# Two of VectorE's weight sums and two of the v transfers in a fused HGRN2 and SwiGLU kernel stand elsewhere

## Chip, core and metric

The kernel runs on one core of a Trainium2 chip. The metric is the device time of one execution in microseconds (us), the median of three runs. The core has five engines that run side by side, each with a queue of its own: TensorE (PE) for matrix products, VectorE (DVE) and ScalarE (ACT) for elementwise work, GpSimd (POOL), which here clears small pieces and issues DMAs, and SyncE (SP), which only issues DMAs. Engines wait for one another by semaphores. On-chip data lie in SBUF, and products arrive in PSUM, in eight banks.

## The reference

Two blocks follow each other. The first is a gated linear recurrence over 768 steps for 4 sequences and 8 heads of size 48; the second is a SwiGLU feed-forward block on the 3072 rows that result.

```python
f = 1.0 / (1.0 + np.exp(-f_logit))
for t in range(S):
    state = f[:, :, t, :, None] * state + np.einsum('bhd,bhe->bhde', k[:, :, t], v[:, :, t])
    y[:, :, t] = np.einsum('bhd,bhde->bhe', q[:, :, t], state)
x = y.transpose(0, 2, 1, 3).reshape(B * S, H * D)     # 3072 x 384
g = x @ w_gate                                        # 384 x 1536
out = (g * (1.0 / (1.0 + np.exp(-g))) * (x @ w_val)) @ w_out
```

Inputs q, k, v and f_logit are float32; the three weight matrices come as 64-bit floats and are turned into 32-bit ones on the chip.

## The kernel before

The 768 steps are cut into six chunks of 128, and a chunk of one sequence is a unit: unit u = 4c + b is chunk c of sequence b. In a unit the recurrence becomes matrix products: scan the gates along the chunk, scale k and q by them, form the scores (k times q, line 666), mask them causally (line 681, tile A), multiply by v (lines 706 and 727, into y), and carry the state on (lines 747 and 756). The feed-forward block runs chunk by chunk too, on the 4 x 128 rows of one chunk. So while the products of chunk c run, the attention of chunk c + 1 is woven in between.

There are three stages. The first does the attention of chunk 0 alone. The middle stage (until about 143 us in the profile) does the feed-forward of chunk 0 plainly (lines 802 and 825) with the attention of chunk 1, and turns the weights into 32 bits piece by piece: w_gate and w_val first, w_out last (join, line 501). The third stage does chunks 1 to 5, each as a block. In a block the hidden layer is computed as a 3 x 3 by 3 x 2 block product with 15 products in the place of 18: `mlp_fifteen` runs the 15 products of `PRODUCTS` four times (line 1004). Groups of products accumulate in one bank each (A, B, o, c). ScalarE copies a bank out between two products of the same letter (line 1009), VectorE adds and subtracts the copies (`plus`, line 905, and `minus`, line 908), ScalarE applies Silu (line 1020), and VectorE multiplies the halves into h (line 956). The copies that VectorE only adds go into three buffers called aside. Then `down_seven` multiplies h by w_out as a 2 x 2 block product with seven products (line 1103 and line 1166). It needs four sums of the halves of w_out, ws1, ws2, w_out's own upper right half, and ws4, which `down_weight_sums` makes once, in the first block of this kind, that is the second of all (chunk 1):

```python
return [lambda: minus(down_sums[1], b12, b11), lambda: minus(down_sums[2], b22, down_sums[1]),
        lambda: minus(b12, b22, b12), lambda: minus(down_sums[4], b21, down_sums[2])]
```

Each is one VectorE operation on 128 x 1152 float32 elements.

In the third stage the order on every engine is the program order, written out by hand: `in_order` at its end ties each engine's instructions together. The order comes from a plan with due times. Each product counts 0.86 of a nominal time unit and each of the seven down products 3.9; a list `waiting` holds the steps of the attention, the sums of tokens and the four weight sums with their due times, and before each product everything that is due is emitted. `DOWN_SUMS_AT` (line 901) holds the due times of the four sums, counted from the start of block 1. The steps of the attention have theirs from `SCORES`, `CHAINS` and `times`. For the unit 9, the gate transpose (line 604) is due at 13.2 and its masks at 26.65; for the unit 10 the gate transpose is due at 28.7. What VectorE has to do with a product's result is emitted one product later (`lag`).

The attention reads its inputs in two ways. Units 0 to 5 load q, k and f in rows and TensorE turns them. From unit 6 on (`by_squares`) the inputs are laid out in 32 x 32 squares, four transfers for each input, which VectorE transposes itself (lines 604, 614, 652). v is always loaded in rows, 128 rows of eight pieces of 48 elements. `load` (line 431) issues the transfers: for chunks 2 and later all from SP; for units 6 and 7, the two units by squares in chunk 1, the squares of f, k and q from GpSimd (line 447) and v from SP (line 454). On SP, v of these units stands among the weight transfers (line 471) and the transfers of y (line 717) of the middle stage. `keep_order(by_pool[-5:])` ties the squares' transfers on GpSimd together.

Of the kernel before, what the change touches and what calls it, by code (L numbers as in the profile page):

```python
# [290 lines left out]
def short_path(ctx, tc, ident, least, judge, q, k, v, f_logit, moe_w_gate, moe_w_val, moe_w_out, out):  # L291
# [9 lines left out]
    nc = tc.nc  # L301
    B, H, S, D = q.shape
# [13 lines left out]
    SQUARES = 2  # L316
# [84 lines left out]
    def by_squares(u):  # L401
        return u >= SQUARES * B - 2
# [6 lines left out]
    def v_of(u):  # L409
        return vs[u % (NV if units[u][1] < SQUARES else NV // 2)]  # L410
# [20 lines left out]
    def load(u, what="fkqv"):  # L431
        b, c = units[u]
        rows = slice(c * C, (c + 1) * C)
        inputs = dict(f=f_logit, k=k, q=q, v=v)
        for nm in "fqkv" if c >= SQUARES else "fvkq" if by_squares(u) else "fkqv":
            src = inputs[nm]
            if nm not in what:
                continue
            if nm == "v":
                dst = v_of(u)  # L440
            elif not by_squares(u):
                dst = raw[nm][u % NRAW]
            else:
                since = len(traced)
                for n in range(4):
                    at = Q * (1 - n % 2)
                    (nc.sync if c >= SQUARES else nc.gpsimd).dma_start(
                        out=rooms[nm][Q * n:Q * (n + 1), at:at + HP * RUN].rearrange("t (a e) -> t a e", a=HP),
                        in_=src[b, n // 2::2, rows, :].rearrange("a (t i) d -> t a (i d)", i=NI))
                if c < SQUARES:  # L450
                    by_pool.extend(ins for ins in traced[since:] if ins.engine == mybir.EngineType.Pool)
                    keep_order(by_pool[-5:])
                continue
            nc.sync.dma_start(out=dst[:, :, 0:D], in_=src[b, :, rows, :].rearrange("h t d -> t h d"))

    def weight_piece(dst, src, parts):

# [97 lines left out]
    def attention(u):  # L555
# [69 lines left out]
        if not in_squares:  # L625
            kp = transposed("kTp", kr)
            qp = transposed("qTp", qr)
            if by_squares(u + 1):
                load(u + 1)
# [120 lines left out]
        if c >= SQUARES and u + 2 < len(units):  # L750
            load(u + 2, "v")
# [7 lines left out]
    def load_after(u, what):  # L759

        if u + 1 < len(units) and u + 1 != SQUARES * B:
            load(u + 1, what)
# [16 lines left out]
    def keep_order(mine):  # L779
        for a, b in zip(mine, mine[1:]):  # L780
            tc.add_manual_dep(b, a.name, mybir.DependencyInfo(mybir.DependencyClass.NoSync,
                                                              mybir.DependencyReason.DATA), reason="order")
# [115 lines left out]
        return {"o": banks_o, "A": banks_a}[kind].tile([128, 512], FP32, tag=kind, name="sc")  # L898

    FINISH = (3, 5, 6, 7, 9, 10)  # L900
    DOWN_SUMS_AT = (28, 34, 38, 48)
    sums = {}

    def plus(dst, a, b):
# [31 lines left out]
    def down_weight_sums():  # L936

        DH = DM // 2
        b11, b12 = w_out[:, 0:NP, 0:DH], w_out[:, 0:NP, DH:DM]
        b21, b22 = w_out[:, NP:NF, 0:DH], w_out[:, NP:NF, DH:DM]  # L940
        for i in (1, 2, 4):
            down_sums[i] = comb.tile([128, NP, DH], FP32, tag=f"ws{i}", name=f"ws{i}")
        return [lambda: minus(down_sums[1], b12, b11), lambda: minus(down_sums[2], b22, down_sums[1]),
                lambda: minus(b12, b22, b12), lambda: minus(down_sums[4], b21, down_sums[2])]
# [364 lines left out]

    waiting += [(at, f) for at, f in zip(DOWN_SUMS_AT, down_weight_sums())]  # L1310
    blocks = {}
# [26 lines left out]
def kernel(  # L1338
# [22 lines left out]
    def judge(bank):  # L1361
# [13 lines left out]
        yield  # L1375

    short_path(tc, ident, least, judge, *args)
    with tc.If(redo[0] > 0, label="redo"):
        general_path(tc, *args)
# [32 lines left out]
```

## Time and profile before

| | |
|---|---|
| median of 3 runs | 604.13 us (604.05 to 604.21) |
| profiled execution | 605.36 us |
| its span, first to last instruction | 603.5 us |
| mean granted TensorE clock | 0.995 |
| second block, 144 to 240 us | VectorE busy 84.0 us, ScalarE 49.0 us |
| VectorE, L908 ws<-w_out and ws<-w_out,ws | 3 operations, 1.33 to 1.35 us each |
| VectorE, L908 w_out<-w_out | 1 operation, 1.35 us |
| v transfers from SP | 24 of 192 KB, 2.7 us from issue to landing (median) |
| squares of f, k, q of units 6 and 7 from GpSimd | 24 of 96 KB |

The span is what the profiler saw between the first and the last instruction; the execution's own time has 1.86 us around it. A row of the order of time gives the start, the duration, the engine, the source line, the operation, the tiles written and read, and in brackets how long the engine sat idle before it and what released it. On VectorE the drawn durations overlap a little: the next operation starts 0.05 to 0.1 us before the drawn end of the one before. The end of a matmul is modelled.

Where the pieces stand in the profile: the four sums start at 176.15, 185.92, 193.30 and 199.84 us; v of unit 6 is issued from SP at 78.20 and v of unit 7 at 99.97. TensorE reads them from 116.65 (unit 6) and 131.00 (unit 7) on.

### The profile page before, as it was taken

Reading aid. Unit: us, or ns where it says so; the run is one execution under the profiler, and the core shown is the slowest. Engines: PE = TensorE matmul, PEld = TensorE weight load, DVE = VectorE, ACT = ScalarE, POOL = GpSimd, SP = SyncE. Lnnn points to the kernel's source line nnn. Section 1 sums busy time; section 2 is a strip of 40 time slices with the busy share of each in tenths; the row PEclk is TensorE's granted clock in tenths of the full one; section 3 lists DMA queues with packets and bytes.
Section 4 is the critical chain, followed back from the end, with each engine's and each line's share of the span. In section 5 each row is a group of like instructions: output and inputs, shape, how many; then the busy total and the mean of one; then the engine's idle time right before and its main releaser. Section 6 shows DMA issues by size and latency. Waiting matters only on the chain.

```text
span 603.5 us, 10851 instructions
## 1 busy us (share of the span) xinstructions
PE 591.9 (98%) x4004; PEld 487.6 (81%) x4004; DVE 480.3 (80%) x831; ACT 294.8 (49%) x559; POOL 86.2 (14%) x199
## 2 busy tenths in 40 slices
PE   7899999999999999999999999999999999999996
PEld 5754545667888899888899888899988899988896
DVE  7999997868999977998895978995878982666631
ACT  2577853215776521567631476742376730356600
POOL 1001251000030150030330030330030320000000
PEclk9999999999999999999999999999999999999999
DMA  9998682015322044342434333343240100100001
GB/s 197 243 294 286 199 211 63 5 35 157 80 63 69 17 129 124 102 114 65 115 103 109 116 91 71 87 110 101 85 105 26 28 9 6 53 1 1 1 1 55
DMA packets 105210, 56.28 MB, mean 93 GB/s; under 512 B 67136, under 2 KB 97216, under 8 KB 105152
## 3 DMA queue, kind: packets, MB, share of 16 engines
q1 hardware_dynamic: 97632, 46.49, 29.4%
q0 software_dynamic: 5504, 6.30, 3.5%
q10 hardware_dynamic: 2016, 2.75, 1.3%
q8 instruction: 32, 0.52, 0.4%
q14 instruction: 26, 0.21, 0.1%
HBM read 45.74 MB, written 6.82 MB: 87 GB/s over the span
## 4 chain that ended last, share of the span: by engine, by line
PE 93%; DVE 5%; issue 1%; ACT 0%; DVEq 0%; ACTq 0%
PE o L1103 19%; PE A L1004 16%; PE B L1004 13%; PE c L1004 5%; PE o L1004 5%; PE gate L802 5%; PE o L825 5%; PE val L802 5%; PE sc L666 4%; PE o L1166 3%; PE y L706 3%; PE y L727 2%; PE dS L747 2%; PE y L702 2%; PE kt L670 1%; DVE c L908 1%
## 5 line engine op out<-in xcount | busy, mean ns | idle before, releaser
L717 POOL DMA_DIRECT2D xT<-yT x120 | 59.9, 507 | 50.3 <-ACT yT L710 45.3
L1103 PE MATMUL o<-w_out,h 128*128 128x192 f32 x360 | 62.0, 327 | 0.5 <-DVE h L956 0.5
L1004 PE MATMUL A<-xs,w_both 128*128 128x256 f32 x240 | 62.2, 382 | 0.0
L1103 PEld LDWEIGHTS o<-w_out,h 128*128 128x128 f32 x360 | 58.7, 190 | 1.7 <-DVE h L956 0.8
L1009 ACT COPY c<-A 128x512 f32<-128x512 f32 x40 | 23.3, 583 | 59.5 <-PE A L1004 59.5
L1009 ACT COPY aside<-A 128x512 f32<-128x512 f32 x60 | 35.1, 586 | 33.7 <-PE A L1004 33.6
L905 DVE TENSOR_TENSOR c<-c,aside 128x512 f32<-128x512 f32 x60 | 41.1, 685 | 12.4 <-ACT aside L1009 11.0
L1004 PEld LDWEIGHTS A<-xs,w_both 128*128 128x128 f32 x240 | 44.9, 190 | 6.6
L956 DVE TENSOR_TENSOR h<-h,c 128x256 f32<-128x256 f32 x100 | 40.4, 412 | 7.3 <-ACT h L1020 7.1
L681 DVE TENSOR_TENSOR A<-sc,causal 128x512 f32<-128x512 f32 x48 | 30.9, 686 | 16.9 <-PE sc L666 16.9
L908 DVE TENSOR_TENSOR c<-c,aside 128x512 f32<-128x512 f32 x60 | 40.9, 682 | 2.8 <-ACT aside L1009 2.8
L1020 ACT ACTIVATE h<-c 128x256 f32<-128x256 f32 x100 | 39.2, 416 | 7.6 <-DVE c L905 5.7
L656 POOL MEMSET gates<- 128x4 f32 x24 | 3.3, 139 | 272.6 <-DVE qT L570 267.5
L1103 PE MATMUL o<-ws,h 128*128 128x192 f32 x240 | 41.5, 328 | 0.2 <-DVE A L681 0.2
L1004 PE MATMUL B<-xs,w_both 128*128 128x256 f32 x160 | 41.3, 380 | 0.1
L1004 PE MATMUL c<-xT,w_both 128*128 128x256 f32 x160 | 41.2, 380 | 0.1
L1004 PE MATMUL A<-xs,extra 128*128 128x256 f32 x160 | 41.2, 380 | 0.0
L1004 PE MATMUL B<-xT,extra 128*128 128x256 f32 x160 | 41.1, 379 | 0.0
L1009 ACT COPY aside<-B 128x512 f32<-128x512 f32 x60 | 35.1, 585 | 9.5 <-PE B L1004 6.6
L1103 PEld LDWEIGHTS o<-ws,h 128*128 128x128 f32 x240 | 39.1, 190 | 0.8 <-DVE A L681 0.4
L905 DVE TENSOR_TENSOR c<-c,o 128x384 f32<-128x384 f32 x15 | 8.3, 552 | 36.3 <-PE o L1103 36.3
L908 DVE TENSOR_TENSOR c<-o,c 128x512 f32<-128x512 f32 x40 | 27.4, 684 | 11.0 <-ACT h L1020 6.2
(149 smaller groups left out, 1221.0 us busy)
## 6 DMA issues: line engine op xcount, KB each, us to landing
fsquares<-in_f_logit_dram SPq DMA_DIRECT2D x64, 96.0 KB, 2.5
qsquares<-in_q_dram SPq DMA_DIRECT2D x64, 96.0 KB, 2.1
ksquares<-in_k_dram SPq DMA_DIRECT2D x64, 96.0 KB, 2.4
v<-in_v_dram SPq DMA_DIRECT2D x24, 192.0 KB, 2.7
w<-in_moe_w_gate_dram SPq DMA_DIRECT2D x6, 768.0 KB, 6.1
w<-in_moe_w_val_dram SPq DMA_DIRECT2D x6, 768.0 KB, 6.2
w<-in_moe_w_out_dram SPq DMA_DIRECT2D x6, 768.0 KB, 5.6
out_dram<-ob ACTq DMA_DIRECT2D x14, 192.0 KB, 2.0
```

The lines of the kernel that those rows point to most:

```text
L666: nc.tensor.matmul(sc[par][:, a * C:(a + 1) * C], lhsT=kT[r, a, :], rhs=qT[r, a, :], start=True, stop=True)
L681: nc.vector.tensor_tensor(A[:, par], sc[par].rearrange("p (a t) -> p a t", t=C), causal.unsqueeze(1).broadcast_to((128, HP, C)), ALU.mult)
L717: (nc.gpsimd if c >= SQUARES else nc.sync).dma_start(out=xT[c][f % 128:f % 128 + n, f // 128, b * C:(b + 1) * C], in_=yT[r:r + n, par, a / ...
L802: nc.tensor.matmul(p, lhsT=w[:, j, i, :], rhs=xT[c][:, i, :], start=(i == 0), stop=(i == KT - 1))
L825: nc.tensor.matmul(p, lhsT=hidden_tile(h, n // 2)[:, n % 2 * 2 + b // 2, b % 2 * C:(b % 2 + 1) * C], rhs=w_out[:, j, :], start=(n == 0), s ...
L905: nc.vector.tensor_tensor(dst, a, b, ALU.add)
L908: nc.vector.tensor_tensor(dst, a, b, ALU.subtract)
L956: lagging.append(lambda: f(*args))
L1004: nc.tensor.matmul(p[name][:, n, :], lhsT=weights_of[a][:, n, j, :], rhs=tokens[b], start=fresh and n == 0, stop=True, skip_group_check=True)
L1009: nc.scalar.copy(t, p[name])
L1020: nc.scalar.activation(dst, src[:, 0, :], AF.Silu)
L1103: nc.tensor.matmul(p[:, n, :], lhsT=lhsTs[j][:, n * C:(n + 1) * C], rhs=rhs[:, j, :], start=first and j == order[0] and n == 0, stop=j == ...
```

## The change

The first two due times of the weight sums become smaller, so that the first sum is emitted directly before the gate transpose of unit 9 and the second directly before the masks of unit 9; the third and fourth stay. And `load` takes GpSimd's queue for v where the unit goes by squares and its chunk is below `SQUARES` (2), that is for units 6 and 7; the order of the transfers in the program is as before (f, v, k, q).

```diff
@@ -451,7 +451,8 @@
                     by_pool.extend(ins for ins in traced[since:] if ins.engine == mybir.EngineType.Pool)
                     keep_order(by_pool[-5:])
                 continue
-            nc.sync.dma_start(out=dst[:, :, 0:D], in_=src[b, :, rows, :].rearrange("h t d -> t h d"))
+            queue = nc.gpsimd if c < SQUARES and by_squares(u) else nc.sync
+            queue.dma_start(out=dst[:, :, 0:D], in_=src[b, :, rows, :].rearrange("h t d -> t h d"))
 
@@ -898,7 +899,7 @@
     FINISH = (3, 5, 6, 7, 9, 10)
-    DOWN_SUMS_AT = (28, 34, 38, 48)
+    DOWN_SUMS_AT = (13.1, 26.5, 38, 48)
     sums = {}
```

## The prediction

> **What bounds the kernel now.** I read the busy times, then the waits of each engine, then the chain of waits, and last the order of time of VectorE (DVE) and TensorE (PE) around the places that the change touches.
>
> ```profile
> PE 591.9 (98%) x4004; PEld 487.6 (81%) x4004; DVE 480.3 (80%) x831; ACT 294.8 (49%) x559; POOL 86.2 (14%) x199
> ...
> 132.00:144.00 12.00, 12.00 (x57) 7.60 (x54) 10.10 (x21) 4.84 (x7) 0.24 (x3) 1.00 0.46 126
> 144.00:240.00 96.00, 95.06 (x701) 84.04 (x700) 84.01 (x140) 49.03 (x99) 15.49 (x35) 1.00 0.34 88
> 240.00:335.00 95.00, 95.00 (x708) 85.05 (x708) 81.76 (x144) 49.11 (x97) 16.53 (x36) 1.00 0.40 104
> ```
>
> TensorE is the bound, so only its holes are worth anything. By stage (start:end, length, busy time of PE, weight loads, DVE, ACT, POOL) it has none from 30 to 144 us and none from 240 to 518 us; outside the first 30 us and the last 85 us, the second block (144 to 240 us) alone has holes, 0.94 us of them. That is also the block of the four sums. The chain of waits shows what makes them:
>
> ```profile
> 186.00 1.25 DVE ws L908
> ...
> 188.28 0.59 ACT aside L1009
> ...
> 188.91 1.13 PE B L1004 x4
> ...
> 194.65 0.61 DVE c L908
> 195.26 0.04 issue
> 195.30 1.15 PE c L1004 x4
> ...
> 203.33 0.61 DVE c L905
> 203.94 0.02 issue
> 203.97 0.43 ACT h L1020
> 204.39 0.02 issue
> 204.41 0.44 DVE h L956
> ...
> 204.90 1.24 PE o L1103 x6
> ```
>
> From about 177.5 to 204.9 us the chain runs almost wholly on VectorE: its queue is behind, and TensorE meets the backlog three times (a bank not yet copied out at 188.91, a bank not yet read at 195.30, a part of h not yet multiplied at 204.90). Products start 0.865 us apart, so B was due at 187.77 + 0.865 = 188.635 and is 0.275 late; c was due at 194.20 + 0.865 = 195.065 and is 0.235 late; the down product was due at 201.59 + 16 x 0.1625 = 204.19 (7.80 us for 48 in the chain gives 0.1625) and is 0.71 late. After each hold the next product starts about 0.10 later than its pace (0.97 for 0.865, as after 188.91). Together 1.22 + 0.30 = 1.5 us: the most that a shorter queue on VectorE can bring here. It is more than the 0.94 of the busy times because part of a hold is drawn as a longer matmul.
>
> ```profile
> 157.94 1.12 DVE L604 STREAM_TRANSPOSE gates<-fsquares 128x512 f32<-128x512 f32 x1 [0.84 <-issue]
> ...
> 174.29 1.29 DVE L681 TENSOR_TENSOR A<-sc,causal 128x512 f32<-128x512 f32 x2 [1.41 <-PE sc L666]
> ...
> 176.15 1.35 DVE L908 TENSOR_TENSOR ws<-w_out 128x1152 f32<-128x1152 f32 x1
> 177.54 0.69 DVE L908 TENSOR_TENSOR c<-o,c 128x512 f32<-128x512 f32 x1
> ```
>
> VectorE is idle 0.84 us before the transpose at 157.94 (it waits for ScalarE's sigmoid, 157.22 to 157.85) and 1.41 us before the masks at 174.29. These are the two places that the sums move to.
>
> **What the Trainium skill says.** "VectorE: DVE Perf Modes", Mode 2×_2P: an operation on two tensors cannot use the second read port to go twice as fast; at the 0.96 GHz of its Specifications 1152 elements are 1.20 us, an estimate. The trace agrees: 1.33 to 1.35 drawn, 1.25 to 1.27 from start to the next start. "TensorE: Matmul & The Clock Gate", Architectural detail: VectorE's queue is strictly first in, first out. So an idle place is filled only by what stands ahead of the waiting instruction, which the gaps above show as well. "SBUF — State Buffer", SBUF: two separate sides: a DMA issued from GpSimd needs descriptors that GpSimd writes, and some VectorE operations keep it from that. The trace fits in size: the same four f transfers took 4.58 us of GpSimd at 58.05 and 2.20 at 78.44. "DMA: Bandwidth & Descriptors", Issuing engines are not separate DMA queues: another issuer saves only issue time; on SP that is 0.42 and 0.53 us for the two v transfers.
>
> **The change part by part.**
>
> *First sum, from 176.15 to ahead of the transpose.* VectorE's operation before it starts at 156.41 and gives way 0.60 later, at 157.01. The sum ends its turn at 158.28 (1.27), so the transpose starts 0.34 late. The next slack is at 163.39, where the addition waits for ScalarE's copy until 163.36; it takes up 0.18 and leaves 0.16. What TensorE needs from this queue next is ScalarE's copy of c at 166.23, held by the h product at 165.74: it would end at 166.98 instead of 166.82, and the product that needs it starts at 167.34. Nothing is lost on TensorE; without the slack at 163.39 the copy ends at 167.16, still in time. Where the sum stood, it is worth almost nothing: it ended at 177.50, and c<-o,c behind it also waits for the product o, which starts at 176.41 and ends 1.03 later, at 177.44. Gain there: at most 0.06, and the h product at 179.09 takes it back, since it starts when ScalarE's Silu ends (178.62 + 0.42 = 179.04).
>
> *Second sum, from 185.92 to ahead of the masks.* VectorE becomes free at 172.80 + 0.16 = 172.96; the sum ends its turn at 172.96 + 1.27 = 174.23, and the scores that the masks wait for come at 174.25. Cost nothing; if the whole 0.34 remained the masks would be 0.12 late, taken up by the idle time that now lies ahead of 177.48. Where it stood it is on the chain, 185.92 to 187.17 = 1.25 us. From there to 203.25 VectorE's starts follow each other at the pace of their kinds (0.60 for 512 elements, 0.33 for 256, 1.27 for the two other sums), so all of it comes 1.25 earlier unless something else is late first.
>
> *What is late next.* I moved the queue of 186 to 205 us forward by hand. ScalarE's copy that held B waits for the addition at 187.50 and for its product (185.91 + 1.03 = 186.94): it starts at 187.03 and ends at 187.62, before 188.635. Product c is due at 194.69; its bank is read out by 194.0. The next copies of A, B and c follow their products with 0.3 us and more to spare. So the first two holds go (0.375 + 0.335 with their restarts) and TensorE reaches the third at 204.19 - 0.71 = 203.48. The part of h comes at 204.90 - 1.25 = 203.65. TensorE still waits 0.17 there, and the gain at that point is VectorE's 1.25, not TensorE's 1.5. Behind it, TensorE, VectorE and ScalarE are all earlier by the same amount; the hold of 0.19 at 221.96 stays, because its mask follows its own scores. From 223 us on nothing holds TensorE, so the 1.25 reaches the end.
>
> *v of the two units.* SP loses two issues of 0.4 to 0.5 us; what follows there (the yT transfers at 93.66 and 117.80) waits for ScalarE. GpSimd gets them:
>
> ```profile
> 58.05 4.58 POOL L447 DMA_DIRECT2D fraw<-in_f_logit_dram  x4 [11.71 <-PE fTp L590]
> 73.62 2.18 POOL L447 DMA_DIRECT2D kraw<-in_k_dram  x4 [11.00 <-PE kTp L590]
> ...
> 87.75 2.34 POOL L447 DMA_DIRECT2D kraw<-in_k_dram  x4 [7.11 <-DVE qT L614]
> ```
>
> The trace has no v on this queue. From below: one issue like the others, 0.55. From above: v has 1024 runs of 192 bytes where one of these transfers has 128 of 768, so eight times 0.55 to 1.15, 4.4 to 9.2 us. A gain is excluded, since TensorE waits for nothing here. I take 2 us; it matters little. The first v falls into GpSimd's 11.00 idle after f; behind it k waits for 73.62 anyway. The second stands between k and q of unit 7, with the clearing of a gate column and nothing else behind; q is read at 110.29, some 14 us after it lands, and v itself at 131. Cost nothing at either end. If the cover were gone, q late by x would cost x less 14, less the 9.3 us between qT (114.2) and its scores (123.5).
>
> Sum: 605.36 (the profiled execution: span 603.5 and 1.86 around it) - 1.25 = 604.1. The median of the three runs lies 1.23 below that execution; the same step from 604.13 gives 602.9.
>
> **The rivals.**
>
> *Something else holds the third and fourth triples.* ScalarE or a buffer takes over part of the 1.25: the two small holds go, the last does not, or the reverse. For it: three holds of different kinds stand within 17 us, and ScalarE's margins are 0.3 to 0.6. Against: every margin I worked out is positive. Gain 0.4 to 0.9: about 603.5.
>
> *All holds go, also the last.* VectorE catches up 0.17 more than its pace shows. Gain 1.5: 602.6.
>
> *Both sums were hidden already.* True of the first, shown above. For the second it would need the h product at 187.17 to wait for ScalarE, whose Silu ended at 184.44: against. 604.1.
>
> *Slower: v's move lays out the middle stage anew.* Between 50 and 144 us the code pins the order of few instructions; the rest is placed by a planner that counts each queue's time. The trace shows that it does not keep program order (two matmuls of y at 112.92, the other fourteen at 116.06). If v's issue on GpSimd pushes the masks of the last unit (done at 127.07) behind later sums, y at 131.00 waits. Cover is 3.9 us; from a slip of 5.2 on the gain is gone. A slip of 7 us, as for ten sums of 0.60 and a join moved ahead, costs TensorE 7 - 3.9 = 3.1 us, less the 1.25 gained: 606.0. Against: v is needed late and no instruction of VectorE depends on it.
>
> **How the numbers follow.** Forecast 0.60, partial gain 0.19, all holds 0.06, nothing 0.05, slower 0.10. About 0.2% (1.2 us) is what a measurement of this kernel can tell from no change, and the forecast's own size, 1.25 with some 0.15 either way from the spacing of VectorE's turns, lies on that edge: I give 0.38 of its 0.60 to faster. Faster 0.38 + 0.06 + 0.02 of the partial = 0.46; slower 0.10; the rest, 0.44, is within. The range 602.3 to 604.4 leaves out the slower case and the tails.
>
> **What would show it.** Right: ws between 157.0 and 158.4 and again between 172.9 and 174.3, no idle time of VectorE at either place, a new one of about 1.3 us ahead of c<-o,c near 177.5; the products near 188.6 and 194.7 at their pace; h and TensorE's down product near 203.65; v on POOL behind f and between k and q. Wrong: a hold of TensorE between 157 and 174 us, a new wait of PE for ACT near 190 to 202, or any hole between 50 and 144 us.

## The result, and the profile after

| | before | after |
|---|---|---|
| median (16 runs of each) | 604.13 us (603.92 to 604.30) | 602.78 us (602.42 to 604.18) |
| ratio of the times | | 0.9982, 95% interval 0.9976 to 0.9989 |
| profiled execution | 605.36 us | 602.79 us |
| span | 603.5 us | 601.1 us |
| granted clock, mean | 0.995 | 0.999 |

The kernel became 1.35 us faster; the forecast was 1.2 faster (602.9). The profiles are 2.57 us apart, which is more than the medians, and the reason lies in the execution that was profiled before, not in the change. In the lines below (start:end, length, busy time of TensorE, weight loads, VectorE, ScalarE, GpSimd, granted clock, DMA) look at the clock, the third figure from the right. First the kernel before, then the kernel after:

```profile
28.00:30.00 2.00, 2.00 (x40) 1.60 (x34) 1.93 (x6) 1.08 (x3) 0.00 (x0) 0.50 0.87 186
30.00:32.00 2.00, 2.00 (x17) 1.27 (x14) 1.74 (x5) 1.47 (x5) 0.00 (x0) 0.65 1.05 333
```

```profile
28.00:30.00 2.00, 1.95 (x49) 1.49 (x50) 1.93 (x5) 1.39 (x4) 0.00 (x0) 1.00 1.03 210
30.00:32.00 2.00, 2.00 (x5) 0.92 (x6) 1.93 (x5) 1.68 (x4) 0.89 (x1) 1.00 0.89 315
```

For about 4 us the matmuls of that one execution ran at half to two thirds of their pace. Two kernels of the experiments below (the two sums alone, the first sum alone) have the same first stage and were profiled without such a dip; in both, the second block starts at 141.85 us, and in the profile of before at 143.20. So the dip cost 1.35 us, about the 1.23 by which the profile of before lay above its median, and which the prediction carried along without a cause. Most variants have some executions that are over 1 us longer at a lower mean clock; they were not profiled, so where their clock dipped is not shown.

So the second block is compared by its length, not by its place. In the chain of waits its first product, A, starts at 143.20 before and at 142.10 after (1.10 earlier), and the attention's y behind the first down products starts at 206.46 before and at 204.09 after (2.37 earlier). The block is 2.37 - 1.10 = 1.27 us shorter. Behind it almost nothing changes up to VectorE's last sum, which starts 2.39 earlier (598.43 and 596.04). Ahead of it something does: with v on SP and no dip the block starts at 141.85, and in the kernel after at 142.10, 0.25 later. That is v's doing, as the experiments show.

The stages of the kernel after, in the same columns:

```profile
144.00:240.00 96.00, 95.80 (x717) 85.20 (x716) 85.19 (x145) 50.65 (x102) 15.47 (x35) 1.00 0.34 85
240.00:335.00 95.00, 95.00 (x697) 85.27 (x697) 81.72 (x144) 47.84 (x96) 16.50 (x36) 1.00 0.40 103
```

The 0.94 us without matmuls in the second block have shrunk to 0.20. The chain of waits of the kernel after shows which are gone (start, length, engine, tile, line; lines are one further down than before):

```profile
187.69 0.86 PE B L1005 x4
188.56 0.86 PE o L1005 x4
...
192.87 0.86 PE B L1005 x4
193.74 0.86 PE c L1005 x4
...
198.91 1.00 PE A L1005 x4
199.91 2.60 PE o L1104 x16
202.51 0.01 issue
202.52 1.57 PE o L1104 x8
...
218.85 0.68 DVE A L682
219.54 0.04 issue
219.58 10.02 PE o L1104 x60
```

The long stretch of VectorE that filled the chain of before between 177.5 and 204.9 us is not there any more: B and c, late by 0.275 and 0.235 before, follow their predecessors at the pace of 0.86, and TensorE alone is the chain up to 218.85, where the mask holds it as it did before. At the down product the view shows no hold, and still a little of one is left. A matmul is drawn about 0.165 us into the next one (four are drawn 1.03 long and follow each other at 0.865), so a hold as short as that leaves no idle time in a view. It is seen by what follows: in the order of time TensorE's 24 down products begin at 199.75 and y at 204.02, 4.27 us for what takes 3.99 without a hold (199.39 to 203.38 in the experiment with three sums below). The 0.28 are the wait of 0.17 and the restart of 0.10 that the prediction left there.

VectorE, in order of time, at the places the sums moved to and the place the first one left:

```profile
155.92 1.35 DVE L909 TENSOR_TENSOR ws<-w_out 128x1152 f32<-128x1152 f32 x1
157.19 1.16 DVE L605 STREAM_TRANSPOSE gates<-fsquares 128x512 f32<-128x512 f32 x1
...
171.89 1.35 DVE L909 TENSOR_TENSOR ws<-w_out,ws 128x1152 f32<-128x1152 f32 x1
173.19 1.29 DVE L682 TENSOR_TENSOR A<-sc,causal 128x512 f32<-128x512 f32 x2
...
176.44 0.69 DVE L909 TENSOR_TENSOR c<-o,c 128x512 f32<-128x512 f32 x1 [1.31 <-PE o L1005]
```

Both sums stand with no idle time of VectorE before or behind them, and the idle 1.31 ahead of c<-o,c is new.

### The profile page after: what moved, and what is told of

Read it like the earlier page. It is cut to its first block, busy times and chain, and to the rows that moved or that the text cites. A ratio compares the mean times of both kernels' runs of the same rounds, so it can differ in the third digit from the quotient of the medians.

```text
span 601.1 us, 10855 instructions
## 1 busy us (share of the span) xinstructions
PE 589.4 (98%) x4004; PEld 486.0 (81%) x4004; DVE 480.5 (80%) x831; ACT 294.7 (49%) x559; POOL 87.7 (15%) x201
## 4 chain that ended last, share of the span: by engine, by line
PE 97%; DVE 1%; ACT 0%; issue 0%; ACTq 0%; DVEq 0%
PE o L1104 20%; PE A L1005 18%; PE B L1005 14%; PE c L1005 6%; PE o L1005 6%; PE gate L803 5%; PE o L826 5%; PE val L803 5%; PE sc L667 4%; PE o L1167 3%; PE y L707 3%; PE y L728 2%; PE dS L748 2%; PE y L703 2%; PE kt L671 1%; PE fTp L591 0%
```

## The experiments

All were timed beside the kernel before on the same chip (604.15, 604.06 and 604.09 us in three sessions, each on another chip). The sums are named by their place in `DOWN_SUMS_AT`.

**The two sums alone, v left on SP.**

```diff
-    DOWN_SUMS_AT = (28, 34, 38, 48)
+    DOWN_SUMS_AT = (13.1, 26.5, 38, 48)
```

> The two sums stand at their new places, v stays on SP. My theory (VectorE's backlog of 186 to 205 us is the whole gain): 602.9, that is 1.25 below before, and TensorE's holds at B and at c of the fourth triple gone. Rival (v brings part of the gain, by the queues of the first 60 us): 603.3 to 604.1.

602.74 us (602.64 to 603.03), ratio 0.9977 (0.9969 to 0.9986). The sums bring the whole gain: 1.41 us here, 1.35 with v on GpSimd.

**v alone.**

```diff
-            nc.sync.dma_start(out=dst[:, :, 0:D], ...
+            (nc.gpsimd if c < SQUARES and by_squares(u) else nc.sync).dma_start(out=dst[:, :, 0:D], ...
```

> v of units 6 and 7 goes from GpSimd, the sums stay where they were. My theory: 604.1, no change within 0.1, since nothing on TensorE waits for these transfers or for GpSimd. Rival (v is part of the gain): 602.9 to 603.7. Rival (v's earlier issue costs something in the crowded first 60 us): 604.4 or more, or more executions with a longer first stage.

603.9 us (603.75 to 607.0), ratio 1.0003 (0.9995 to 1.0011): no effect on the time that can be told. But the order of time shows that v is not where the prediction put it, and that its issue is not free. The kernel before, then v alone:

```profile
25.66 0.36 DVE L498 TENSOR_SCALAR top<-top 128x384 int32<-128x384 int32 x1
...
27.02 1.28 DVE L681 TENSOR_TENSOR A<-sc,causal 128x512 f32<-128x512 f32 x2
...
27.59 0.43 SPq L454 DMA_DIRECT2D v<-in_v_dram  x1
...
27.80 1.84 PE L727 MATMUL y<-A,v 128*32 128x128 f32 x32 [0.64 <-issue]
```

```profile
24.95 1.16 POOL L454 DMA_DIRECT2D v<-in_v_dram  x1 [4.49 <-PE dS L747]
25.29 0.35 DVE L496 TENSOR_SCALAR top<-top 128x384 f32<-128x384 f32 x1
...
25.67 0.60 DVE L498 TENSOR_SCALAR top<-top 128x384 int32<-128x384 int32 x1
...
27.28 1.28 DVE L681 TENSOR_TENSOR A<-sc,causal 128x512 f32<-128x512 f32 x2
...
28.07 1.19 PE L727 MATMUL y<-A,v 128*32 128x128 f32 x31 [0.90 <-ACT kt L679]
```

While GpSimd issues v of unit 6 (1.16 us), one VectorE operation beside it, of a weight piece, takes 0.60 instead of 0.36. The queue behind it is 0.25 late, with the masks and so the product y. (The trace puts y's wait down to ScalarE's kt, done at 27.85; the masks are what comes last.) The page "SBUF — State Buffer" of the Trainium skill states in its section Who interferes with whom that VectorE's modes with two ports, which operations of this kind (TENSOR_SCALAR) can enter, and GpSimd contend for a shared pair of ports: whoever starts first has it for the whole instruction, and the other blocks. The trace agrees in part: the operation that was held ends 0.16 after GpSimd's, but the one before it (25.29), which also started during the issue, was not held. That GpSimd's issue causes the delay is shown by the runs with one v each, below; that the ports are the way is not. The prediction had taken from that page only the other direction, VectorE keeping GpSimd waiting.

**The first sum alone.** `DOWN_SUMS_AT = (13.1, 34, 38, 48)`, v on SP.

> Only the first sum moves, ahead of the gate transpose; the second stays due at 34. My theory: the first sum was hidden behind the wait for product o, so 604.0 to 604.1, and the idle time of about 1.3 us ahead of c<-o,c near 177.5 shows it. Rival (each sum is worth half): 603.5.

604.14 us, ratio 1.0003 (0.9995 to 1.0011). VectorE's order of time there:

```profile
176.20 0.69 DVE L908 TENSOR_TENSOR c<-o,c 128x512 f32<-128x512 f32 x1 [1.31 <-PE o L1004]
```

The sum has gone, and VectorE stands idle for its whole length in the same place, since c<-o,c cannot start before the product o. TensorE is busy 20.25 of the 21 us from 185 to 206, as before. The first sum was hidden where it stood.

**Both sums directly ahead of the masks.** `DOWN_SUMS_AT = (26.4, 26.5, 38, 48)`, v on SP.

> Both sums stand directly ahead of the masks (due 26.4 and 26.5), none at the transpose. The gap there is 1.41 us and the two need 2.5, so the masks come 1.05 late, near 175.3; the wait for product o until 177.48 takes that up. My theory: 602.9, as with both moves. Rival (the place ahead of the transpose is needed for the first sum): 603.5 to 604.1.

602.84 us (602.64 to 603.14), ratio 0.9976 (0.9967 to 0.9985): as good as the change. VectorE, in order of time:

```profile
171.49 1.35 DVE L908 TENSOR_TENSOR ws<-w_out 128x1152 f32<-128x1152 f32 x1
172.87 1.36 DVE L908 TENSOR_TENSOR ws<-w_out,ws 128x1152 f32<-128x1152 f32 x1
174.15 1.28 DVE L681 TENSOR_TENSOR A<-sc,causal 128x512 f32<-128x512 f32 x2
...
176.23 0.69 DVE L908 TENSOR_TENSOR c<-o,c 128x512 f32<-128x512 f32 x1
```

The masks are 1.2 later than with the two places of the change (172.95) and take up the idle 1.31 that the first sum left behind; c<-o,c is where it was. So the place ahead of the transpose isn't needed. The second sum was not moved by itself; but both together gain 1.41 or 1.31 and the first alone nothing, so what counts is that the second leaves the stretch from 186 us on.

**The second sum done twice.** The kernel before, with the second sum repeated where it stands (the same values are written a second time).

```diff
-    waiting += [(at, f) for at, f in zip(DOWN_SUMS_AT, down_weight_sums())]
+    at_sums = list(zip(DOWN_SUMS_AT, down_weight_sums()))
+    waiting += at_sums + [(34.1, at_sums[1][1])]
```

> The kernel before, with the second sum done twice, one behind the other, at its old place. My theory: between 186 and 205 us TensorE follows VectorE's queue, so a sum more costs what a sum less gains: 1.25, so 605.4. Rival (the queue has slack that one more sum only uses up): 604.1 to 604.6.

605.5 us (605.26 to 606.62), ratio 1.0026 (1.0015 to 1.0037): 1.44 longer than before. TensorE, in order of time:

```profile
188.94 1.13 PE L1004 MATMUL B<-xs,w_both 128*128 128x256 f32 x4 [1.51 <-ACT aside L1009]
```

Product B, 0.275 late before, now waits 1.51 us, by the way the prediction named: sum, h and addition on VectorE, the copy of the bank on ScalarE, the product. A sum at this place costs about its own length of 1.25, taken away or added.

**The third sum moved as well.** `DOWN_SUMS_AT = (13.1, 26.5, 28, 48)`, v on SP, so that w_out's sum stands in the idle time that the first sum opened.

> Sums at their new places, v on SP, and the third sum is due at 28, in the idle time ahead of c<-o,c that the first one left. My theory: it fits there (1.27 into 1.31), VectorE's queue of 186 to 205 us is shorter by another 1.25, TensorE's last hold (0.17 and 0.10 with its restart) goes and nothing else is gained: 602.45, 0.27 below the sums alone. Rival (VectorE still sets the end of the block): 601.5. Rival (the sum pushes the gate transpose behind it): 602.7 or more.

602.5 us (602.25 to 604.66), ratio 0.9980 (0.9972 to 0.9987). VectorE and then TensorE in order of time, and the busy times by stage:

```profile
174.68 1.35 DVE L908 TENSOR_TENSOR w_out<-w_out 128x1152 f32<-128x1152 f32 x1
176.08 0.69 DVE L908 TENSOR_TENSOR c<-o,c 128x512 f32<-128x512 f32 x1
```

```profile
199.39 4.06 PE L1103 MATMUL o<-w_out,h 128*128 128x192 f32 x24
203.38 0.67 PE L702 MATMUL y<-qT,decayed 48*64 48x128 f32 x16
```

```profile
185.00:206.00 21.00, 21.00 (x147) 18.38 (x147) 20.07 (x34) 12.82 (x27) 0.11 (x1) 1.00 0.07 20
```

The third sum fills 1.3 us in which VectorE waited, the last of the three holds goes, and with it the 0.28 that were left. By the medians three sums are the fastest: 1.56 us below the kernel before, where the two sums alone are 1.41 and the change 1.35 below. The intervals overlap, so the size of this last step rests on the trace. A second timing, in another session, gave 602.58 (1.51 below; ratio 0.9973, 0.9964 to 0.9983):

> The same three sums with v on SP, for the comparison on one chip: 602.5 in both theories, y at 27.8, the window 185 to 206 us full on TensorE.

**v of one unit alone,** with the two sums of the change: `nc.gpsimd if u == 7`, and `nc.gpsimd if u == 6`.

> Sums at their new places, and only v of unit 7 goes from GpSimd. Seen so far: v of unit 6 is issued by GpSimd at 24.95 us for 1.16 us, and a VectorE operation at 25.67 takes 0.60 in the place of 0.36, so TensorE's y near 27.8 starts 0.25 later. My theory now: GpSimd's descriptor work for v of unit 6 holds VectorE, v of unit 7 (issued near 30.2) holds nothing that matters. So here y starts at 27.8, the last sum of VectorE at 595.8 as with the sums alone, time 602.7. Rival (any v on GpSimd costs, or gains, alike): y or the first stage moves here too.

> Sums at their new places, and only v of unit 6 goes from GpSimd. My theory: the VectorE operation at 25.67 takes 0.60, y starts at 28.05, the last sum stands at 596.0, all as in the changed kernel; time 602.7 to 602.9, and more executions with a dip of TensorE's granted clock near 28 us (1.2 us longer), since TensorE is idle 0.25 longer just ahead of it. Rival (the dips fall by chance): as rare as with the sums alone.

Unit 7 alone: 603.2 us (602.93 to 605.15); VectorE's operation at 25.65 takes 0.36 and y starts at 27.81, as before the change. Unit 6 alone: the operation takes 0.60 and y starts at 28.05. So v of unit 6 is what holds y. (Beside unit 7's issue a VectorE operation is longer too, 0.78 instead of 0.36 us at 30.36, but y is under way by then.) The times don't fit as well. Unit 7 alone is about 0.5 longer than the two sums alone, which were timed on another chip. Of unit 6 alone seven of 13 executions were 1.1 us or more above the rest, which makes its median 604.33, and the rest (603.09 to 603.25) is also 0.4 longer, though VectorE's last sum starts at 596.03, as in the change (596.04). From that sum to the end of the span the profiles have 4.8 to 5.6 us, another length in each kernel; part of the 0.4 lies there. What sets that end is open.

**Three sums with both v on GpSimd,** beside the same without.

> The third sum moved as well, with v of units 6 and 7 on GpSimd; the kernel beside it has the same sums with v on SP. Theory one (GpSimd's work for v of unit 6 holds a VectorE operation of the first stage by 0.24 us and with it y at 27.8): y about 0.25 later than in the kernel beside it, and a median 0.2 to 0.3 longer, 602.7 to 602.8 against 602.5, with more executions in which the granted clock dips near 28 us. Theory two (v costs nothing, as predicted): the same median within 0.1 and the same share of dips.

602.49 us (602.25 to 603.51), ratio 0.9971 (0.9960 to 0.9982), against 602.58. y starts at 28.06 and not 27.82, as the first theory says, but the median doesn't show it: of three pairs with and without v on GpSimd (change and sums alone 602.78 and 602.74, in different sessions; v alone and before 603.9 and 604.15; this pair) none is longer by more than 0.04. The profiles do show it up to VectorE's last sum. Here are the first sum alone, whose time is that of the kernel before and whose profile has no dip, and v alone:

```profile
597.08 0.35 DVE L905 TENSOR_TENSOR ob<-c,o 128x192 f32<-128x192 f32 x1 [1.59 <-PE o L1166]
```

```profile
597.36 0.35 DVE L905 TENSOR_TENSOR ob<-c,o 128x192 f32<-128x192 f32 x1 [1.59 <-PE o L1166]
```

With v on GpSimd the last sum is 0.28 later; between the sums alone and the change it is 0.22 (595.82 and 596.04), and in this pair 0.63. What comes behind the last sum is shorter with v on GpSimd in the first pair (5.22 and 4.84 us) and in this one (5.47 and 4.94) and takes most of it back; in the second (5.08 and 5.06) it is not, and there the profiled executions are 0.15 apart (602.64 and 602.79). In this kernel's profiled execution, 602.86 us long, TensorE also has one wait in the middle stage, which makes up the rest of the 0.63:

```profile
PE sc L667 <- ACT top L491: 0.3, 1, 0.3
```

The scores of unit 5 at 78.24 come behind a weight piece of ScalarE. Unit 7 alone had the same wait with 0.15, the change and unit 6 alone have none. Whether v causes it, by what it moves among the weight transfers, was not separated.

## Why the prediction was right, and where it was not

*The bound and the three holds.* Right. The gain is all in the second block, and the two holds that the forecast said would go are gone. One reading was off: the three holds, 1.22 together, show as less idle time not because a held matmul is drawn longer, but because each matmul of these products is drawn 0.165 into the next, so each hold shows about 0.16 less (0.11, 0.07 and 0.55; with the later 0.19 these are the 0.94 within 0.02).

*First sum, nothing; second sum, 1.25.* Right; the first is shown alone, the second by the difference and by doubling it. The first leaves 1.31 us of idle time ahead of c<-o,c, as foretold; the second costs 1.44 when doubled and, with the first, 1.41 when moved. The block itself became 1.27 shorter. The place ahead of the transpose, whose delay of 0.34 was to be absorbed, did no harm and was not needed.

*What is late next.* Right: no wait of TensorE for ScalarE came near 190 to 202 us, and the third hold remained with 0.28 for 0.17 + 0.10. The rival in which all holds go, put at 0.3 us more than the forecast, is what the third sum brought about.

*v of the two units.* The median shows no loss, as forecast; the steps were wrong, and the trace does show a small loss. First, the place. The page of before has v issues from SP at 78.20 and 99.97, and I took these for units 6 and 7; they are units 8 and 9. With v of both units on GpSimd the issues at 78.22 and 100.02 are still on SP, and those that are gone are the ones of 27.59 and 55.89, which were v of units 6 and 7. The buffers come free when the products of units 2 and 3 have read them, and the planner takes the transfer as early as that. GpSimd now issues them at 24.94 and 30.18 us, not behind f at 62 and k at 90. What was said of the idle times there bears on nothing. Second, the price. The "2 us" taken for an issue measured 1.16 and 0.89, within the bounds. Third, "cost nothing at either end" left out that an issue of GpSimd can hold VectorE: it cost y 0.25 us in the first stage, where TensorE does wait, and 0.22 of that are still there at VectorE's last sum. I had excluded a hole only after 50 us. That this didn't reach the median has nothing to do with the prediction's cover.

*How near the number came.* In part by luck. At VectorE's last sum the kernel after is 1.04 us ahead of the kernel with the first sum alone (597.08 and 596.04): 1.26 for the second sum, less 0.22 for v. The medians of these two are 1.36 apart (604.14 and 602.78). So about 0.3 of the gain lies behind the last sum, with nothing that explains it, and makes up for the v that was put at nothing. Each of these starts is from one profiled execution.

*The slower rival.* Its mechanism didn't appear: on TensorE and ScalarE the two programs have the same order, on VectorE only the two sums stand elsewhere, and TensorE is busy without a break from 34 to 143 us. v went earlier, not into the stretch where the masks of the last unit had 3.9 us of cover.

*The profile and the median.* Carrying the same step over from 605.36 to 604.13 was sound, since the clock's dip of before lies outside the block.

## What to carry to other kernels

On an engine whose queue is behind, an operation costs its length only in the stretch where the backlog reaches the bound engine; move it past the nearest wait ahead of that stretch, and then see what idle time it leaves behind, since the next operation fits there (here the third sum, for 0.28 us more). Look up where a transfer is issued by its buffer's readers, not by the first issue of that name that fits: a planner that issues early may have put it in another stage. And before two profiles are subtracted, compare the granted clock by stretches of a few us.

## What was not expected of the hardware

A DMA's issue on GpSimd lengthened a VectorE operation of another buffer from 0.36 to 0.60 us. Beside the second issue, in the kernel after, the same pair shows again, one held and one not (columns as before):

```profile
30.18 0.89 POOL L455 DMA_DIRECT2D v<-in_v_dram  x1 [3.88 <-PE dS L748]
30.22 0.35 DVE L497 TENSOR_SCALAR top<-top 128x384 f32<-128x384 f32 x1
...
30.61 0.62 DVE L499 TENSOR_SCALAR top<-top 128x384 int32<-128x384 int32 x1
```

With v of unit 7 alone the issue (29.94, 1.05 long) makes the same operation 0.78 long. In all three issues the held operation ends 0.15 or 0.16 us after the drawn end of the issue, whatever its length, as if it had waited for that end. The operation that is not held (float32) always comes earlier in the issue, 0.34 us or less behind its start, and the held one (int32) 0.42 or more. Whether the kind of operation or the moment decides was not separated.

TensorE's granted clock fell to 0.50 near 28 us in the profiled execution of before, though the longest idle time of TensorE in the 8 us ahead of it was 0.79 us. The Trainium skill ("TensorE: Matmul & The Clock Gate", What's actually happening) gives half clock as the state after an idle window of about 3.4 us. The half fits; the idle window isn't there. Executions more than 1 us above the lowest of their kernel (38 in all, 37 of them with a mean clock of 0.992 to 0.997, where all other executions have 0.997 to 1.000) were 19 of 58 where v of unit 6 is issued from GpSimd and 19 of 202 where it is not. The later y, a longer pause of TensorE just there, may be the link, but the three-sum pair had 1 of 7 and 1 of 10, and no profile of a dipped execution with v on GpSimd was taken; the cause is open.
